# One more gate/up tile moved out of the attention filler, a thinner filler from unit 14 on, and three DMA issues moved, in a transformer block on one Trainium2 core

## The chip, the cores and the metric

The kernel runs on one core of a Trainium2 chip. The metric is the device time of one execution in microseconds. Before the change three runs gave 1046.39, 1044.46 and 1044.87 us, so the median is 1044.87 us. Engines are named as in the profile: PE (TensorE matmuls), PEld (its weight loads), DVE (VectorE), ACT (ScalarE), POOL (GpSimd) and SP (SyncE, here only the issuer of most DMAs).

## What is computed

x is 2048 tokens by 640 features in float32. After a layer norm, two branches run on the same normed x, and both are added to x:

```
xn  = layernorm(x)
A   = softmax(q k^T / sqrt(20), causal, window 256) v @ wo     # 32 heads of 20
B   = (gelu(xn @ w_gate) * (xn @ w_up)) @ w_down               # 640 -> 1728 -> 640
out = x + A + B
```

## The kernel before, in words

Nearly every dense product is done as three float32r products of split operands (high by high, low by high, high by low), so a product of 128 output rows by 512 tokens over 640 features is 15 matmuls. Tokens are cut into 4 chunks of 512. The gate and up weights are cut into 14 tiles of 128 columns; tile 13 holds the last 64 columns of both.

The program has three long stages, each with an order written out by hand.

**Attention (`attention`, L818).** Heads go in 8 groups of four, so there are 32 units (group, chunk). Each unit is 14 slots. In a slot a fixed pattern puts instructions out: `exp_piece` (L558) in every odd slot up to 11, two pieces at a time, computes scores on PE into the tile `ps_e` (pool `psx`, two buffers, shared with `ps_o`) and ACT takes the exponential out of it (L574); `max_pair` (L488) in slots 0, 0 again, 5 and 9 computes scores for a coming unit on PE into `ps_m` (pool `psm`, four buffers), and DVE scans them for row maxima (L517); `av_unit` (L593) in slot 0 multiplies the probabilities of the unit before by v into `ps_o`, and ACT copies it out (L621, L622); POOL clears the masked parts of the probabilities (L587, L590). `max_end` (L531) comes in slot 7: it turns the row maxima of the next unit by a matmul (`ps_n`, L534), ACT copies them to `mr` (L536), and a DMA on ACT's queue writes them as two more rows of the query tile `qs` (L537), which the next unit's `exp_piece` reads as part of its contraction from its slot 1 on.

The rest of PE's time in a slot is filled from a generator, `filler` (L705), which gives out matmuls of other work one by one: the remaining q and k projections (`proj_qk`, L240), the v projections (`proj_v`), and whole gate/up tiles (`gate_up_fill`, L661). A 512-column matmul counts 1, a 320-column one 0.65. `pull_fill(RATE / NS)` (L863) takes 30.9 of them per unit, 2.2 per slot. `sets` (L700) lists what the filler holds: q/k tiles 1 to 4, then gate/up tiles 0, 1 and 2 (`range(1, NFA)` with `NFA = 3`); tile 13 is loaded with it and multiplied just behind the attention. A filler gate/up tile is 2 x 15 x 4 = 120 matmuls. Its followers are ACT's L669, L670 and L679, and DVE's L675, L683 and L690, placed a few slots behind by `defer` and by the table `LAG`; a q/k tile has L277, L273, L255 and L259 as its followers.

**Gate/up (`gate_up_pair`, L954).** The tiles from `NFA` on are done here, each in two calls, one per pair of chunks. A call uses sums of token chunks and of weights, which leave 54 matmuls of 512 columns per call, 108 per tile. The attention's leftovers (normalising its output, sums of down-projection weights) are worked off in between by `work` (L1121).

**Down and output projection (from L1414).** 8 token blocks of 256, each with 9 weight quads and one remainder step. `fetch` (L1031) loads a weight quad into `stg`; after the first ones it is issued by ACT, from the table `plan` (L1425). `load_step` issues the loads of activations on SP, four steps ahead; `drain` (L1262) adds the products to x and stores a block through SP, which issues in order.

Of the kernel before, what the change touches and what calls it, by code (L numbers as in the profile page):

```python
# [28 lines left out]
SR = 3 * DH  # L29
QROWS = 64 + SR  # L30
NS = 14
RATE = 30.9
LAST = 8
V1_SLOT = 169
MXD = 7
KSLOT = 9
LAG = 3, 5, 4, 4, 4, 4, 3, 3, 4, 3, 2, 1, 1, 1
NFA = 3
HD = D // 2
HR = 5  # L40
NQD = 9
# [26 lines left out]
def block_kernel(ctx, tc, x, wqk, wv, wgu, wdo, wdl, out):  # L68
    nc = tc.nc
# [128 lines left out]
    now = [None]  # L198

    def at(slot, fn, *a):  # L200
        acts.setdefault(slot, []).append((fn, a))
# [3 lines left out]
    def late(fn, *a):  # L205
        if now[0] is None or now[0] < NS:
            fn(*a)
        else:
            lates.append((fn, a))
# [6 lines left out]
    def lag():  # L216
        return 1 if now[0] is None or now[0] < NS else LAG[now[0] % NS]

# [119 lines left out]
    NQ, NK = 3, 4  # L338
    qs = [st1.tile([128, 4, C], BF, name=f"qs{i}") for i in range(NQ)]
# [191 lines left out]
    def max_end(u):  # L531
        nm = maxes.pop(u)
        ps = psm.tile([128, 128], F32, name="ps_n", tag="mx")
        nc.tensor.matmul(ps, nm.rearrange("p z a j b -> p (z a j b)"), identb, start=True, stop=True)  # L534
        mr = ap.tile([32, 128], BF, name="mr", tag="mr")
        nc.scalar.activation(mr, ps[0:32], AF.Copy)  # L536
        late(lambda: nc.scalar.dma_start(qs[u % NQ][SR:SR + 2].rearrange("p j t -> p (j t)"), mr))  # L537

    def pieces(c):
        b = 4 * c  # L540
# [159 lines left out]
    sets = [("qk", 1), ("qk", 2), ("qk", 3), ("qk", 4), ("gu", 0)]  # L700
    sets += [("gu", f) for f in range(1, NFA)] + [("gu", NF - 1)]
    pools = (wp, None), (hp, 2)
# [110 lines left out]
    def pull_fill(n):  # L813
        debt[0] += n
        while debt[0] > 0:
            debt[0] -= next(fill, 1.0)

    def attention():  # L818
        now[0] = -1
        load_stack(0)  # L820
        load_stack(1)
        load_stack(2)
        for i, (p, k, half) in enumerate((p, k, half) for p in range(NC // 2) for k in range(2) for half in range(2)):
            for j, fn in enumerate(x_sums(p, k, half)):
                m = 10 * i + j
                at(NS * (XS0 + m // XSN) + m % XSN, fn)
        for i in range(12):
            now[0] = i - 13
            for fn, a in tick():
                fn(*a)  # L830
            if i == 0:
                pull_max(1, now[0])
                pull_fill(RAMP)
                pull_max(1, now[0])
                debt[0] -= RAMP
            elif i % 2 == 0:
                pull_max(2, now[0])
            flush()
            pull_fill(2 * RAMP)
        pull_fill(GAP)  # L840
        for u in range(NU + 1):
            for i in range(NS):
                T = now[0] = NS * u + i
                for fn, a in tick():
                    fn(*a)
                if i in (0, 5, 9) or T == 3:
                    pull_max(2, T)
                if i == 0 and u:
                    if u == NU:
                        pull_fill(LAST)  # L850
                    av_unit(u - 1)
                    flush()
                    pull_max(2, T)
                if i % 2 and i < 12 and u < NU:
                    exp_piece(u, i - 1)
                    if i == 1 and u:
                        pull_fill(1)
                        debt[0] -= 1
                    exp_piece(u, i)
                flush()  # L860
                if u + 3 < NU and i in (KSLOT, 12):
                    load_stack(u + 3, (int(i == KSLOT),))
                pull_fill(RATE / NS)  # L863
        while acts:
            now[0] += 1
            for fn, a in tick():
                fn(*a)
            flush()
        now[0] = None
        run(fill)  # L870
        assert not acts
# [156 lines left out]
    def four(t):  # L1028
        return t.rearrange("p k (h n) -> p (k h) n", h=2)

    def fetch(kind, q, where="stg", eng=nc.sync):  # L1031
        if where == "wr":
            ts = [wrp.tile([128, KT, 128], F32, name="wr", tag="wr").rearrange("p k m -> p (k m)") for _ in range(2)]
        elif where != "stg" and where != "at":
            ts = [tp.tile([128, D], F32, name=f"b{n}{q}", tag=f"x{n}{where}") for n in "hl"]
        if where != "stg" and where != "at":
            for i, t in enumerate(ts):
                nc.sync.dma_start(t, wdo[q][:, i])
            staged[kind, q] = [(t.rearrange("p (h n) -> p h n", h=2), slice(2 * i, 2 * i + 2)) for i, t in enumerate(ts)]
            return  # L1040
        pool, bufs = (rp3, 3) if where == "stg" else (cp, 3)
        t = pool.tile([128, 4, HD], F32, name="stg", tag=where, bufs=bufs)
        eng.dma_start(t, four(wdo[q]) if kind == "b" else wtd[q])
        if kind == "t" and q in borrow:
            staged[kind, q] = [(t[:, i:i + 1], slice(i, i + 1)) for i in range(4)]
        else:
            staged[kind, q] = [(t, slice(0, 4))]
# [95 lines left out]
    NP = S // 256  # L1143
# [118 lines left out]
    def drain(p, ps, xt):  # L1262
        xs = {(r, h): xt[:, 2 - r, h * HD - HD:h * HD] for r in (1, 2) for h in (1, 2)}
        rows = {1: slice(256 * p + 128, 256 * p + 256), 2: slice(256 * p, 256 * p + 128)}

        def add(r, h, i, eng=nc.vector):
            eng.tensor_tensor(out=xs[r, h], in0=i, in1=xs[r, h], op=OP.add)  # L1267

        def store(r, h=None):
            cs = slice(h * HD - HD, h * HD) if h else slice(0, D)  # L1270
            nc.sync.dma_start(out[rows[r], cs], xt[:, 2 - r, cs])

        b = {i: ps[i][:, 0:HD] for i in ps}
        if p == 0:
            for bank, r, h in ((2, 1, 1), (3, 1, 2), (4, 2, 1), (8, 2, 2)):
                add(r, h, b[bank])
                if h == 2:
                    store(r)
            return
        a = copies.pop(p)  # L1280
        both = cp.tile([128, 2, HD], F32, name="u2", tag="r13")
        q, c5 = both[:, 0], both[:, 1]
        if p < NP - 1:
            nc.scalar.activation(c5, b[5], AF.Copy)
        if p == NP - 1:
            add(1, 1, b[2])
            add(1, 1, a)
            store(1, 1)
            sub(q, b[6], a, OP.add)
            add(1, 2, q)  # L1290
            sub(q, b[7], q, OP.add)
            add(2, 1, q)
            add(2, 2, q)
            add(2, 1, b[4])
            store(2, 1)
            add(1, 2, b[5])
            add(2, 2, b[5])
            store(2, 2)
            add(1, 2, b[3])
            store(1, 2)  # L1300
            return
        add(2, 1, b[4])
        sub(q, b[6], a, OP.add)
        add(1, 2, q)
        sub(q, b[7], q, OP.add)
        add(1, 2, b[3])
        add(1, 2, c5)
        add(1, 1, a)
        store(1)
        add(2, 1, q)  # L1310
        add(2, 2, c5)
        add(2, 2, q)
        if p == 1:
            add(2, 2, b[8])
        store(2)
# [7 lines left out]
    order.__enter__()  # L1323
    raws_w = load_gu(NFA)
    banks = [psg.tile([128, C], F32, name="ps_g", tag=f"g{i}") for i in range(4)]
# [104 lines left out]
    def prepare(n):  # L1430
        for op in plan.get(n, "").split():
            kind, q = op[1], int(op[-1])
            if op[0] == "f":
                fetch(kind, q, eng=nc.scalar)
            elif op[0] == "s":
                sum_quad(q)
            elif op[0] == "p":
                kind, q, i = "t", int(op[1]), int(op[2])
                for raw, t, dst in parts(kind, q):
                    raw, dst = (raw, dst) if q in borrow else (raw[:, i:i + 1], slice(i, i + 1))  # L1440
                    if q not in borrow or t is quads["b", borrow[q] + i]:
                        nc.scalar.activation(t[:, 0, dst], raw, AF.Copy)
                        sub(t[:, 1, dst], raw, t[:, 0, dst].bitcast(F32))
            else:
                (high_quad if op[0] == "h" else low_quad)(kind, q)
        if n == 2:
            nc.scalar.activation(w13[:, 0], raw13, AF.Copy)
            sub(w13[:, 1], raw13, w13[:, 0].bitcast(F32))
        if n == 0:
            fetch("b", 5)  # L1450
            fetch("b", 6)
# [76 lines left out]
```

## Time and profile before

| what | us |
|---|---|
| median of three runs | 1044.87 |
| the profiled execution, device time | 1045.72 |
| its span in the trace | 1044.0 |
| PE busy | 1033.4 |
| DVE busy | 741.7 |
| ACT busy | 527.5 |
| POOL busy | 385.5 |

The profiled execution is 0.85 us over the median, and 1.7 us of its device time lie outside its span. A line of the timeline reads: start, duration, engine, source line, operation, output tile <- input tiles, shape, count, and in square brackets the idle time before it with what ended that. Matmul durations overlap: one row's duration is not the step from one matmul to the next, which is read from the starts. A line of the chain reads: start, duration, what, count.

### The profile page before, as it was taken

Reading aid. Unit: us, or ns where it says so; the run is one execution under the profiler, and the core shown is the slowest. Engines: PE = TensorE matmul, PEld = TensorE weight load, DVE = VectorE, ACT = ScalarE, POOL = GpSimd, SP = SyncE. Lnnn points to the kernel's source line nnn. Section 1 sums busy time; section 2 is a strip of 40 time slices with the busy share of each in tenths; the row PEclk is TensorE's granted clock in tenths of the full one; section 3 lists DMA queues with packets and bytes.
Section 4 is the critical chain, followed back from the end, with each engine's and each line's share of the span. In section 5 each row is a group of like instructions: output and inputs, shape, how many; then the busy total and the mean of one; then the engine's idle time right before and its main releaser. Section 6 shows DMA issues by size and latency. Waiting matters only on the chain.

```text
span 1044.0 us, 25563 instructions
## 1 busy us (share of the span) xinstructions
PE 1033.4 (99%) x9393; PEld 834.3 (80%) x9393; DVE 741.7 (71%) x2018; ACT 527.5 (51%) x1120; POOL 385.5 (37%) x623
## 2 busy tenths in 40 slices
PE   9999999999999999999999999999999999999998
PEld 8887666666777666666678888888888999999998
DVE  7755666677655676677736778776555889888887
ACT  4534766767666666666675322233224554433332
POOL 5122788888755787766461111101110000000000
PEclk9999999999999999999999999999999999999999
DMA  5552356554633354343325576662216874433333
GB/s 211 180 157 70 110 157 183 165 181 142 183 98 100 114 168 138 103 134 110 99 77 193 188 244 212 253 250 105 78 59 242 263 249 136 138 127 123 117 121 106
DMA packets 102150, 158.74 MB, mean 152 GB/s; under 512 B 14172, under 2 KB 55260, under 8 KB 102024
## 3 DMA queue, kind: packets, MB, share of 16 engines
q1 hardware_dynamic: 99640, 150.94, 44.5%
q10 hardware_dynamic: 2384, 6.16, 1.7%
q8 instruction: 74, 1.21, 0.5%
q14 instruction: 52, 0.43, 0.1%
HBM read 101.78 MB, written 54.92 MB: 150 GB/s over the span
## 4 chain that ended last, share of the span: by engine, by line
PE 90%; DVE 5%; ACT 2%; DMA 2%; issue 1%; POOL 0%; ACTq 0%; DVEq 0%; SPq 0%
PE ps_g L972 22%; PE ps_d L108 20%; PE ps L1244 20%; PE ps_e L572 8%; PE ps_v L108 7%; PE ps_o L615 5%; PE ps_m L507 5%; DVE junk L517 2%; PE ps_g L108 1%; DMA stg<-wdo 1%; ACT wb L1058 1%; PE ps_d L356 1%; PE ps_t L185 0%; DVE wb L1077 0%; DMA qs<-qd 0%
## 5 line engine op out<-in xcount | busy, mean ns | idle before, releaser
L517 DVE CUSTOM_DVE_ANT_0 junk<-ps_m,mask 128x320 bf16<-128x320 f32 (+2 forms) x512 | 243.0, 475 | 128.9 <-PE ps_m L507 71.0
L574 ACT ACTIVATE P<-ps_e 128x512 f32<-128x512 f32 (+2 forms) x384 | 198.7, 572 | 68.3 <-PE ps_e L572 67.8
L1244 PE MATMUL ps<-wb,at 128*128 128x320 f32 x999 | 156.4, 309 | 0.8 <-DVE xr L1267 0.8
L1244 PEld LDWEIGHTS ps<-wb,at 128*128 128x128 f32 x999 | 148.9, 188 | 1.5 <-issue 1.0
L587 POOL TENSOR_SCALAR_AFFINE_SELECT P<-P 128x256 f32<-128x256 f32 (+1 forms) x192 | 94.5, 494 | 73.2 <-ACT P L574 70.0
L572 PE MATMUL ps_e<-qs,ks 124*128 124x128 bf16 (+2 forms) x704 | 118.3, 278 | 0.1
L108 PE MATMUL ps_d<-xh,wqh 128*128 128x512 f32 x310 | 99.0, 422 | 0.2 <-ACT xh L193 0.2
L108 PE MATMUL ps_d<-xl,wqh 128*128 128x512 f32 x310 | 98.5, 422 | 0.0
L108 PE MATMUL ps_d<-xh,wql 128*128 128x512 f32 x310 | 97.6, 418 | 0.0
L101 POOL TENSOR_TENSOR wql<-wr,wqh 128x640 fp32r<-128x640 f32 x12 | 19.2, 1608 | 195.6 <-PE ps_g L972 171.1
L1244 PE MATMUL ps<-wt,at 128*128 128x320 f32 x552 | 88.9, 309 | 0.0
L572 PEld LDWEIGHTS <-ks 124*128 124x128 bf16 x704 | 49.5, 98 | 49.0 <-issue 33.4
L1244 PEld LDWEIGHTS ps<-wt,at 128*128 128x128 f32 x552 | 82.9, 188 | 0.1
L590 POOL TENSOR_SCALAR_AFFINE_SELECT P<-P 128x512 f32<-128x512 f32 (+1 forms) x144 | 76.7, 541 | 16.2 <-ACT P L574 16.2
L1198 ACT ACTIVATE at<-ss 128x512 fp32r<-128x512 f32 x59 | 37.3, 632 | 84.5 <-DVE ss L1077 84.5
L615 PE MATMUL ps_o<-P,v 64*32 64x320 f32 (+4 forms) x2816 | 74.2, 347 | 0.0
L259 POOL TENSOR_TENSOR pt<-r,pt 128x512 bf16<-128x512 f32 x40 | 46.8, 1169 | 64.6 <-ACT pt L255 57.0
L615 PEld LDWEIGHTS ps_o<-P,v 64*32 64x32 f32 x2816 | 50.8, 106 | 21.5 <-issue 0.9
L507 PE MATMUL ps_m<-ks,qs 60*64 60x320 bf16 (+3 forms) x1472 | 64.6, 260 | 3.4 <-DVE mx L517 1.5
L108 PEld LDWEIGHTS ps_d<-xh,wqh 128*128 128x128 f32 x310 | 56.0, 189 | 10.4 <-issue 1.6
L507 PEld LDWEIGHTS <-qs 60*64 60x64 bf16 x1472 | 29.1, 105 | 43.8 <-issue 35.6
L108 PEld LDWEIGHTS ps_d<-xh,wql 128*128 128x128 f32 x310 | 56.0, 189 | 10.1 <-issue 0.9
(195 smaller groups left out, 1967.4 us busy)
## 6 DMA issues: line engine op xcount, KB each, us to landing
hd<-he SPq DMA_DIRECT2D x50, 256.0 KB
hr<-hd SPq DMA_DIRECT2D x48, 256.0 KB
wr<-wgu SPq DMA_DIRECT2D x27, 320.0 KB
qs<-qd SPq DMA_DIRECT2D x64, 120.0 KB
ks<-kd SPq DMA_DIRECT2D x64, 120.0 KB
xi<-x SPq DMA_DIRECT2D x16, 320.0 KB
qs<-qd SPq DMA_DIRECT2D x64, 80.0 KB
ks<-kd SPq DMA_DIRECT2D x64, 80.0 KB
```

The source lines that it names most:

```text
L108: nc.tensor.matmul(ps, a(k), b(k), start=n == 0, stop=n == 3 * nk - 1)
L259: nc.gpsimd.tensor_tensor(out=pt[:, l, :], in0=r, in1=pt[:, 1, :], op=OP.subtract)
L507: nc.tensor.matmul(ps[64 * h:64 * h + 64, col:col + w], q[rows, j, q0:q0 + 64], ks_, start=True, stop=True, tile_position=(64 * r, 64 * h))
L517: nc.vector.tensor_tensor_reduce(out=junk[:, 0:n], in0=ps[:, 320 - n:320], in1=mask[:, 320 - n:320], scale=1.0, scalar=NEG, op0=OP.add, op ...
L572: nc.tensor.matmul(ps[:, col:col + n], k[0:QROWS, j, kc:kc + 128], q[0:QROWS, j, q0:q0 + n], start=True, stop=True)
L574: nc.scalar.activation(pt[:, j, lo:hi], ps[:, lo:hi], AF.Exp, scale=SCALE)
L587: nc.gpsimd.affine_select(out=a, in_=a, pattern=[[0, n], [1, 128]], compare_op=OP.is_ge, fill=0.0, base=0, channel_multiplier=-1)
L590: nc.gpsimd.affine_select(out=a, in_=a, pattern=[[0, n], [-1, 128]], compare_op=OP.is_ge, fill=0.0, base=-1, channel_multiplier=1)
L615: nc.tensor.matmul(os[r][32 * j:32 * j + 32, qa:qb], v[rows, w0_:w0_ + 32], pt[rows, j, col + qa - q0:col + qb - q0], start=r not in begun ...
L972: nc.tensor.matmul(ps, i, j, start=first and n == 0, stop=n == len(work) - 1, skip_group_check=True)
L1198: nc.scalar.activation(hi[:, 3:7], s, AF.Copy)
L1244: nc.tensor.matmul(ps[bank][:, 0:HD], *work[bank][j], start=bank not in begun, stop=final[p, bank] == n and j == len(work[bank]) - 1, skip ...
```

## The change

Three things change. First, `NFA` goes from 3 to 2: gate/up tile 2 leaves the filler and is done by `gate_up_pair`, as the first of 11 tiles there instead of 10; with 120 matmuls less to give out, the filler's rate goes from 30.9 to 24.2 per unit from unit 14 on. Second, the DMA of the maxima row is put in slot 13 of the unit, instead of slot 7. Third, in the last stage the quads listed in `plan` are fetched by GpSimd and not by ACT, and the stores of `drain` are issued by GpSimd and not by SP, but for the last block.

```diff
+TURN, RATE2 = 14, 24.2
...
+MRSLOT = 13
...
-NFA = 3
+NFA = 2
...
-        late(lambda: nc.scalar.dma_start(qs[u % NQ][SR:SR + 2].rearrange("p j t -> p (j t)"), mr))
+        issue = lambda: nc.scalar.dma_start(qs[u % NQ][SR:SR + 2].rearrange("p j t -> p (j t)"), mr)
+        if now[0] < 0:
+            issue()
+        else:
+            at(now[0] - now[0] % NS + MRSLOT, issue)
...
-                pull_fill(RATE / NS)
+                pull_fill((RATE if u < TURN else RATE2) / NS)
...
-            nc.sync.dma_start(out[rows[r], cs], xt[:, 2 - r, cs])
+            (nc.sync if p == NP - 1 else nc.gpsimd).dma_start(out[rows[r], cs], xt[:, 2 - r, cs])
...
-                fetch(kind, q, eng=nc.scalar)
+                fetch(kind, q, eng=nc.gpsimd)
```

Lines of the changed kernel stand 2 to 6 lines lower than those of before; L574 is L580 there, L108 is L110, L537 is L539.

On PE, in a unit of the second half, this is the piece from the last score product of slot 5 to the first of slot 7 before (`ps_e` are the score products, `ps_d` the filler, `ps_n` the turned maxima):

```order
L572 LDWEIGHTS ks_182
L572 MATMUL ps_e<-qs_178,ks_182 128x256
L108 MATMUL ps_d<-xh_79,wqh 128x512 x5
L534 LDWEIGHTS nm_183
L534 MATMUL ps_n<-identb,nm_183 128x128
L572 LDWEIGHTS ks_181
L572 MATMUL ps_e<-qs_178,ks_181 128x256
```

And the same piece in a unit of the changed kernel's second half:

```order
L578 LDWEIGHTS ks_182
L578 MATMUL ps_e<-qs_178,ks_182 128x256
L110 MATMUL ps_d<-xl_80,wqh 128x512 x2
L110 MATMUL ps_d<-xh_77,wqh 128x512
L536 LDWEIGHTS nm_183
L536 MATMUL ps_n<-identb,nm_183 128x128
L578 LDWEIGHTS ks_181
L578 MATMUL ps_e<-qs_178,ks_181 128x256
```

Three filler matmuls stand between the two pairs of score products in this place, where five stood; in other units there are four before, or four after.

On ACT, a whole unit of the second half before reads as follows, from the copies of `ps_o` in slot 0 to the unit's end (`P` are the exponentials, `gs` and `he` the followers of a filler gate/up tile):

```order
L621 ACTIVATE ob<-ps_o 128x512
L622 ACTIVATE P<-ps_o 128x512
L574 ACTIVATE P<-ps_e 128x384 x4
L574 ACTIVATE P<-ps_e 128x256 x2
L536 ACTIVATE mr<-ps_n 32x128
L574 ACTIVATE P<-ps_e 128x256 x2
L537 DMA qs_178<-mr 2x16x128
L574 ACTIVATE P<-ps_e 128x512 x2
L669 ACTIVATE gs<-ps_d 128x512
L670 ACTIVATE he<-ps_d 128x512
L574 ACTIVATE P<-ps_e 128x512 x2
L679 ACTIVATE he<-he 128x512
```

And a unit of the changed kernel's second half:

```order
L627 ACTIVATE ob<-ps_o 128x512
L628 ACTIVATE P<-ps_o 128x512
L580 ACTIVATE P<-ps_e 128x512 x6
L538 ACTIVATE mr<-ps_n 32x128
L580 ACTIVATE P<-ps_e 128x512 x2
L675 ACTIVATE gs<-ps_d 128x512
L676 ACTIVATE he<-ps_d 128x512
L580 ACTIVATE P<-ps_e 128x512 x4
L685 ACTIVATE he<-he 128x512
L539 DMA qs_176<-mr 2x16x128
```

The DMA of the maxima row stands behind all the exponentials of the unit, and `gs` and `he` stand before four exponentials where two were left. A gate/up chunk is 30 filler matmuls: at 30.9 per unit its followers come at nearly the same slot in every unit, at 24.2 the slot changes from unit to unit.

On ACT, the first fetches of the last stage stand before among the splits of weights (`wb`, `wt`) and of activations (`at`):

```order
L1043 DMA stg<-wdo 128x1280
L1058 ACTIVATE wb_12653<-stg 128x1280
L1058 ACTIVATE wt_12655<-stg 128x1280
L1186 ACTIVATE at<-hr 128x512
L1043 DMA stg<-wtd_112 128x1280
L1043 DMA stg<-wtd_114 128x1280
L1058 ACTIVATE wb_12692<-stg 128x1280
```

On POOL, the changed kernel's program ends with these, where before it had nothing behind the splits of the gate/up stage:

```order
L1049 DMA stg<-wdo 128x1280 x2
L1049 DMA stg<-wtd_112 128x1280
L1049 DMA stg<-wtd_114 128x1280
L1049 DMA stg<-wtd_113 128x1280
L1049 DMA stg<-wtd_108 128x1280
L1277 DMA out<-xr 128x640 x2
L1049 DMA stg<-wtd_109 128x1280
L1049 DMA stg<-wtd_110 128x1280
L1049 DMA stg<-wtd_111 128x1280
L1277 DMA out<-xr 128x640 x12
```

Nine fetches and fourteen stores thus wait in one queue in which nothing else stands.

## The prediction

> **What bounds the kernel now.** I read the page's busy times first, then the stages as windows, then the chain that ended last, and the waits in the stage that the change thins out.
>
> ```profile
> span 1044.0 us, 25563 instructions
> PE 1033.4 (99%) x9393; PEld 834.3 (80%) x9393; DVE 741.7 (71%) x2018; ACT 527.5 (51%) x1120; POOL 385.5 (37%) x623
> PEclk9999999999999999999999999999999999999999
> ```
>
> PE is busy for 99% of the span, at a clock granted in full all the way. Rows of matmuls overlap, so 99% could hide small gaps; the stages and the steps between matmuls say more. The windows are the attention's units 1 to 13, its units 14 to 31, the gate/up stage and the last stage (columns: window, its length, PE, PEld, DVE, ACT, POOL busy, clock, DMA share, GB/s).
>
> ```profile
> 102.10:287.10 185.00, 183.82 (x2452) 123.72 (x2448) 125.22 (x466) 126.99 (x270) 150.32 (x254) 1.00 0.54 159
> 287.10:541.00 253.90, 252.19 (x3395) 173.81 (x3394) 163.37 (x602) 168.18 (x373) 171.40 (x293) 1.00 0.37 113
> 543.40:802.10 258.70, 258.70 (x1146) 213.97 (x1141) 177.24 (x294) 85.27 (x157) 28.93 (x20) 1.00 0.51 178
> 802.10:1044.00 241.90, 237.77 (x1616) 236.75 (x1614) 206.70 (x443) 100.25 (x179) 0.00 (x0) 1.00 0.47 159
> ```
>
> The second window holds the 18 units that get less filler: 253.9 / 18 = 14.1 us each. In it DVE, ACT and POOL are busy for 64%, 66% and 68%, so none of them is the bound on average. The steps of the matmuls come from the chain:
>
> ```profile
> 50.30 6.85 PE ps_d L108 x30
> ...
> 557.27 234.08 PE ps_g L972 x1032
> ...
> 835.99 204.71 PE ps L1244 x1391
> ```
>
> A filler matmul takes 6.85 / 30 = 0.228 us, a gate/up one 234.08 / 1032 = 0.2268 us, one of the last stage 0.1472 us. The last two rows are runs of hundreds of microseconds in which PE waits for nothing, so time leaves those stages only with matmuls. Next, the waits in the 18 units (who waits, for whom, total us, times, longest):
>
> ```profile
> PE ps_m L507 <- DVE mx L517: 1.1, 4, 0.4
> ACT P L574 <- PE ps_e L572: 40.8, 68, 1.5
> ACT ob L621 <- PE ps_o L615: 33.6, 16, 3.5
> ```
>
> PE is recorded as waiting 1.1 us there, always for DVE's scan of a maxima tile. ACT waits for PE, 40.8 us for scores alone. So this stage is bound by PE's own work, with cover for the other engines: 2.3 us per unit before ACT's exponentials.
>
> **Part 1: the tile.** Out of the filler go 2 x 15 x 4 = 120 matmuls at 0.228 us: -27.4 us, if PE stays the bound. Into the gate/up stage come 108 at 0.2268 us: +24.5 us. That stage runs as one chain of PE, and DVE has 81 us of idle time in it (258.70 - 177.24), so followers, sums and DMAs of the extra tile lie beside PE. Net -2.9 us. The tile's fetches by SP, its splits on ACT and POOL and its four stores go with it, into a stage where POOL is 11% and ACT 33% busy.
>
> **Part 2: what the thinner filler uncovers.** A unit should shrink from 14.1 us by 6.7 x 0.228 = 1.5 us to 12.6 us. DVE, 163.37 / 18 = 9.1 us per unit, POOL 9.5 and ACT 9.3 still fit, even before the tile's followers go out. So no engine takes over on average; the question is the short distances. The score pieces have two buffers, and these rows of PE, and of ACT below it, show how near they are:
>
> ```profile
> 482.81 0.61 PE L572 MATMUL ps_e<-qs,ks 124*128 124x128 bf16 x4
> 483.13 0.77 PE L108 MATMUL ps_d<-xl,wqh 128*128 128x512 f32 x2
> 483.74 0.62 PE L108 MATMUL ps_d<-xh,wqh 128*128 128x512 f32 x2
> 484.20 0.63 PE L572 MATMUL ps_e<-qs,ks 124*128 124x128 bf16 x4
> ```
> ```profile
> 483.31 1.09 ACT L574 ACTIVATE P<-ps_e 128x512 f32<-128x512 f32 x2 [1.08 <-PE ps_e L572]
> 484.28 0.60 ACT L669 ACTIVATE gs<-ps_d 128x512 f32<-128x512 f32 x1
> 484.76 0.62 ACT L670 ACTIVATE he<-ps_d 128x512 f32<-128x512 f32 x1
> 485.23 1.12 ACT L574 ACTIVATE P<-ps_e 128x512 f32<-128x512 f32 x2
> ```
>
> Two pieces start on PE at 482.81, ACT reads them from 483.31 to 484.40, and PE starts the next two at 484.20, 1.39 us after the first. The second of these needs the buffer that ACT lets go at 484.40, and begins half-way through a pair's 0.33 us, at about 484.36. So four filler matmuls between two pairs just cover ACT. With three, PE comes 0.23 us sooner and waits some 0.2 us. In the changed order such gaps (slots 5 to 7 and 9 to 11) have three or four, 24.2 / 7 = 3.46 on average, so about half are short: 2 x 0.5 x 0.2 = 0.2 us per unit. The gaps with `ps_m` in them (3 to 5, 7 to 9) are some 0.4 us longer and stay covered; slots 1 to 3 add at most 0.1 us. Upper end 0.3 x 18 = 5.4 us. Lower end 0: a wait moves the second piece back, which gives ACT the same time before the next pair, and the 40.8 us of waiting ACT say that it catches up. I take 0.15 us per unit, half of the upper end, because the only row of such a gap lies right on the edge: +2.7 us.
>
> Second, `gs` and `he` hold ACT for 0.95 us (484.28 to 485.23). Before, they come as here, ahead of a unit's last two exponentials or behind them, where no later score piece waits. In the changed order they drift: in a few units of the tail they stand ahead of four or six exponentials. A wrong place costs between 0 (a gap with `ps_m` behind it) and 0.75 us (0.95 less the 0.2 by which a short gap, 1.39 - 0.23, exceeds two exponentials, 0.97), over 8 chunks 0 to 6 us; ACT's idle share makes me put most of it inside the 2.7 us, and the rest into a rival.
>
> DVE's four recorded waits, 1.1 us, depend on the same drift; I keep them (bounds -1.1 to +2).
>
> **Part 3: the maxima row.** The DMA leaves ACT's row between two exponentials and stands where ACT waits for `ps_o` anyway. The gain is nothing that PE sees. The risk is its distance to its reader, shown by PE's rows from slot 0 to slot 1:
>
> ```profile
> 472.12 0.37 PE L507 MATMUL ps_m<-ks,qs 60*64 60x64 bf16 x12
> ...
> 475.76 0.39 PE L572 MATMUL ps_e<-qs,ks 124*128 124x128 bf16 x2
> ```
> ```profile
> SPq L482 <- DMA qs<-mr: 9.2, 6, 2.5
> ```
>
> From the scan products of slot 0 to the first score piece are 3.64 us, and slot 13's filler adds 0.3 to 0.5 us. SP was held by this DMA for at most 2.5 us at a time. So it arrives with over a microsecond in hand; I take 0, with bounds of 0 and, were half of the 32 units late by 0.5 us, +8 us. Nothing is queued behind it but the copies of `ps_o`, and it waits for an `mr` that was written six slots before.
>
> **Part 4: the last stage's issues.**
>
> ```profile
> 817.65 0.40 ACTq L1043 DMA_DIRECT2D stg<-wdo  x1
> ...
> 823.45 1.26 ACT L1058 ACTIVATE wb<-stg 128x1280 fp32r<-128x1280 f32 x1
> ...
> 827.05 1.74 ACTq L1043 DMA_DIRECT2D stg<-wtd  x2
> 828.84 1.27 ACT L1058 ACTIVATE wb<-stg 128x1280 fp32r<-128x1280 f32 x1 [1.99 <-DVE wt L1077]
> ```
> ```profile
> 835.99 14.31 PE L1244 MATMUL ps<-wb,at 128*128 128x320 f32 x96 [0.81 <-DVE xr L1267]
> ```
> ```profile
> SPq L1271 <- DVE xr L1267: 100.0, 12, 12.5
> ```
>
> ACT stands for 1.99 us behind two fetches that wait for a staging buffer; the split of a quad, DVE's low part and then DVE's additions `xr` come that much later, and PE waits 0.81 us for the first of them. On GpSimd, idle in this stage, the fetches hold up nobody. That can return the 0.81 us, and SP's loads no longer stand behind stores (100 us of waiting), which PE doesn't feel, since it has no other wait here. I take -0.8 us; ends -1.0 and, if a load by GpSimd comes late, +3. A fetch issued at 817.65 is read without a wait 5.8 us later, so there is room for a slower issue.
>
> The Trainium skill speaks against this part: its page DMA: Bandwidth & Descriptors, section Issuing engine by pattern, gives simple loads and stores to SP, and the section Latency and other measured facts puts the first byte of a GpSimd DMA at about 1 us against 0.6 us for one of SP or ACT. By that page the 0.8 us would be an estimated 0.4 us. No trace here shows a DMA of GpSimd.
>
> **The sum.** 1045.72 - 27.4 + 24.5 + 2.7 + 0 - 0.8 = 1044.7 us against the profiled execution, -1.0 us. That execution is 0.85 us over the median, so the forecast for the median is 1043.9 us.
>
> **The rivals.**
> - *All of it is covered*: ACT's 40.8 us and the alternation keep PE from waiting. Then -2.9 - 0.8 = -3.7, with DVE's waits gone too -4.8: about 1040.7 us. For it: PE hardly waits in the units now. Against it: the gap at 484.20 has no slack.
> - *The score buffers become the bound* (slower): short gaps and drifting `gs`/`he` add up in the 18 units. Price 5.4 us plus half of the 6 us, with -3.7: +4.7, 1049.6 us. It decides from 0.32 us of new waiting per unit on (5.8 us in all, 3.7 to undo the gain and 2.1 to pass 0.2%). For it: ACT's row in the changed order; against it: 34% idle time of ACT.
> - *A late DMA* (slower): the maxima row after its 4 us, or a fetch by GpSimd after its 5.8 us: +3 to +8 us, some 1049 us.
> - *The tile isn't cheaper where it goes* would need a wait in the gate/up stage, which has none: left out.
>
> **How the numbers follow.** The forecast, 1042.5 to 1046 us, has 0.44; everything covered 0.29; score buffers 0.19; late DMA 0.08. The range of 1040.0 to 1049.2 us takes in the forecast, the covered case and the nearer half of the slower ones. A measurement of this kernel can tell about 0.2% (2.1 us) from no change: faster means under 1042.8, slower over 1047.0. The covered case is faster, with a little of the forecast: 0.36. The two slower cases and a little of the forecast: 0.26. The rest, 0.38, is the same.
>
> **What would show it.** Right: the run of L978 in the chain has 108 more matmuls at 0.227 us; the units from 14 on take 12.6 to 12.9 us; waits of `ps_e` for ACT of 0.1 to 0.3 us each, two or so per unit; PE's wait at the start of the second token block of the last stage is gone. Wrong: units of 13 us or more, a PE wait for `qs<-mr` at slot 1, ACT waiting for `stg` behind a GpSimd issue, or units at 12.6 us without any waits (then the covered case holds).

## The result and the profile after

The changed kernel is slower. Its median is 1058.58 us of five runs (1054.95 to 1060.53), beside 1044.95 us for the kernel before in the same series; the ratio is 1.0119, with a 95% interval of 1.0101 to 1.0136. The forecast was 1043.9 us, with a range that ended at 1049.2 us. The profiled execution took 1060.53 us. Of the five runs the one with a mean granted clock of 1.0 took 1054.95 us and the four at 0.996 to 0.998 took 1057.18 to 1060.53 us; a run of e7 at 0.753, 1250.09 us long, is in no ratio below.

The first lines of its page:

```profile
span 1058.7 us, 25550 instructions
...
PE 1040.7 (98%) x9381; PEld 836.7 (79%) x9381; DVE 747.2 (71%) x2029; ACT 527.2 (50%) x1120; POOL 393.4 (37%) x638
...
PEclk9999999999999999999999999999999999999999
```

PE has 12 matmuls less in this execution and is busy 7.3 us longer. The digit row of the clock looks as before, but a slice is 26 us long and hides what is shown below. The same four stages as windows (units 1 to 13, units 14 to 31, gate/up, last stage; columns: window, length, PE, PEld, DVE, ACT, POOL busy, clock, DMA share, GB/s):

```profile
102.10:297.20 195.10, 188.16 (x2452) 126.24 (x2448) 125.87 (x467) 127.56 (x270) 149.79 (x254) 0.98 0.52 151
297.20:532.70 235.50, 231.59 (x3263) 153.44 (x3259) 154.11 (x590) 160.45 (x359) 165.80 (x286) 1.00 0.39 115
535.10:818.20 283.10, 283.10 (x1259) 234.48 (x1250) 193.00 (x319) 92.58 (x172) 31.15 (x21) 1.00 0.50 170
818.20:1058.70 240.50, 237.19 (x1616) 236.69 (x1614) 205.20 (x441) 99.87 (x179) 12.57 (x23) 1.00 0.49 158
```

Against the windows of before that is +10.1, -18.4, +24.4 and -1.4 us, +14.7 in all, the difference of the spans. The tile costs in gate/up what it was to cost, the thinner units give back less than they were to (18.4 of 27.4 us), and 10 us are lost in units 1 to 13, where only the maxima row was moved. Two of these units make 8.1 of the 10.1 us: unit 5 takes 19.32 us instead of 15.15, unit 9 takes 18.15 instead of 14.17. The chain that ended last names that loss, here first that of before and then that of after (`qs<-qd` is the load of the queries of a unit, with the keys `ks<-kd` its stack loads; the scan products that read them first go into `ps_m`):

```profile
162.23 4.11 DMA qs<-qd
```
```profile
149.61 2.17 DMA qs<-qd
...
165.72 3.30 DMA qs<-qd
...
226.69 3.19 DMA qs<-qd
...
258.71 2.22 DMA qs<-qd
...
286.48 2.95 DMA qs<-qd
...
549.03 269.28 PE ps_g L978 x1188
818.30 237.09 PE ps L1250 x1615
```

Before, one stack load stands in the chain of these units; after, PE's end hangs on five. The gate/up row has 1188 matmuls instead of 1032 at 269.28 / 1188 = 0.2267 us (the run of the chain begins at another place than before, so that its count grows by more than the 108 of the tile), so the price of a gate/up matmul has not changed.

**Where the 10 us are made.** The timeline around 160 us: the DMA issues of SP, in the second fence that of ACT, in the third PE.

```profile
156.45 2.33 SPq L484 DMA_DIRECT2D ks<-kd  x6
161.17 0.83 SPq L236 DMA_DIRECT2D wr<-wqk  x2
162.11 1.33 SPq L270 DMA_DIRECT2D qd<-pt  x2
163.54 2.89 SPq L484 DMA_DIRECT2D qs<-qd  x6
```
```profile
158.47 0.62 ACTq L539 DMA_DIRECT2D qs<-mr  x1
```
```profile
167.68 0.27 PE L509 MATMUL ps_m<-ks,qs 60*64 60x256 bf16 x1 [1.83 <-DMA qs<-qd]
169.16 0.47 PE L509 MATMUL ps_m<-ks,qs 60*64 60x256 bf16 x15 [1.22 <-DMA qs<-qd]
```

SP has put out six loads by 158.78 and then stands until 161.17, though the next two loads (`wr`) have nothing to do with the maxima row. The rows of SP's program say why:

```
184 L636 DMA sd_99<-ob 4x512 [waits DMAHW7_49]
185 L484 DMA ks_182<-kd_91 40x1024 [waits DMAHW0_49]
...
190 L484 DMA ks_182<-kd_91 60x1024 [waits DMAHW5_49]
191 L236 DMA wr<-wqk 128x640 [waits DMAHW6_49]
```

In this program, as it is built, the DMAs of SP and ACT share eight completion semaphores and take them in turn, one round of eight after the other. The one that SP skips ahead of row 184 was given to ACT's maxima row, and row 191, eight places on from ACT's row in that round, may not be issued until that DMA has landed. ACT issues the row at 158.47; SP comes to row 191 at 158.78, long before the row has landed, and stands until 161.17. Behind it stand the `qd` stores and the `qs` loads, which come some 2 us later than before (the last is issued by 166.4 instead of 164.4), and PE waits 1.83 and 1.22 us for them. Then something happens that the row of digits doesn't show: windows just before and just behind these waits, and at the second such place.

```profile
165.70:169.60 3.90, 0.85 (x18) 0.45 (x18) 0.77 (x2) 1.57 (x3) 2.23 (x4) 1.00 0.77 227
169.60:173.00 3.40, 3.40 (x16) 2.32 (x14) 1.92 (x8) 1.99 (x5) 1.59 (x2) 0.50 0.43 129
231.10:234.50 3.40, 3.40 (x12) 2.37 (x11) 1.43 (x6) 2.71 (x6) 1.29 (x2) 0.50 0.19 62
```

For 3.4 us PE gets half its clock, which costs another 1.7 us at each of the two places. The waits of units 1 to 13, of SP's queue and of PE:

```profile
SPq L484 <- DMA qs<-mr: 15.8, 8, 3.3
...
SPq L270 <- DMA qs<-mr: 2.4, 1, 2.4
...
SPq L236 <- DMA qs<-mr: 2.4, 1, 2.4
```
```profile
PE ps_m L509 <- DMA qs<-qd: 5.9, 7, 1.8
...
PEld L578 <- DMA qs<-mr: 0.3, 1, 0.3
```

The same waits of these units before the change:

```profile
SPq L482 <- DMA qs<-mr: 7.6, 4, 2.5
```
```profile
PE ps_m L507 <- DMA qs<-qd: 0.6, 1, 0.6
```

SP waits 20.6 us for the row instead of 7.6; for the row itself PE's weight load waits 0.3 us, and the product not at all. So the row is not late for its reader. What it holds up is SP.

**Where the thinner units lose.** A short gap of unit 24, between two pairs of score pieces, now with three filler matmuls:

```profile
436.37 0.61 PE L578 MATMUL ps_e<-qs,ks 124*128 124x128 bf16 x4
...
436.68 0.53 PE L110 MATMUL ps_d<-xl,wqh 128*128 128x512 f32 x1
...
436.86 1.09 ACT L580 ACTIVATE P<-ps_e 128x512 f32<-128x512 f32 x2 [1.04 <-PE ps_e L578]
...
437.05 0.63 PE L110 MATMUL ps_d<-xh,wqh 128*128 128x512 f32 x2
...
437.52 0.85 PE L578 MATMUL ps_e<-qs,ks 124*128 124x128 bf16 x4
```

The pairs start 1.15 us apart instead of 1.39. ACT lets the second buffer go at 436.86 + 1.09 = 437.95, and the second pair lasts 0.85 us instead of 0.61: a wait of 0.24 us, too short for the view of waits, which has only a fraction of this loss.

### The profile page after: what moved, and what is told of

Same layout as the page of the kernel before. It is cut to its first block, busy times and chain, and to the rows that moved or that the text cites. A ratio compares the mean times of both kernels' runs of the same rounds, so it can differ in the third digit from the quotient of the medians.

```text
span 1058.7 us, 25550 instructions
## 1 busy us (share of the span) xinstructions
PE 1040.7 (98%) x9381; PEld 836.7 (79%) x9381; DVE 747.2 (71%) x2029; ACT 527.2 (50%) x1120; POOL 393.4 (37%) x638
## 4 chain that ended last, share of the span: by engine, by line
PE 90%; DVE 4%; ACT 3%; DMA 2%; issue 1%; SPq 0%; POOL 0%; DVEq 0%; ACTq 0%
PE ps_g L978 25%; PE ps L1250 22%; PE ps_d L110 16%; PE ps_e L578 8%; PE ps_v L110 6%; PE ps_o L621 6%; PE ps_m L509 5%; DVE junk L519 2%; ACT P L580 2%; DMA qs<-qd 2%; PE ps_g L110 1%; PE ps_d L358 1%; PE ps_t L187 0%; DMA xi<-x 0%; SPq L484 0%
## 5 line engine op out<-in xcount | busy, mean ns | idle before, releaser
L580 ACT ACTIVATE P<-ps_e 128x512 f32<-128x512 f32 (+2 forms) x384 | 198.7, 572 | 60.3 <-PE ps_e L578 59.0
L578 PE MATMUL ps_e<-qs,ks 124*128 124x128 bf16 (+2 forms) x704 | 123.7, 280 | 2.3 <-ACT P L580 0.7
L110 PE MATMUL ps_d<-xh,wqh 128*128 128x512 f32 x270 | 90.0, 430 | 0.2 <-ACT xh L195 0.2
L110 PE MATMUL ps_d<-xl,wqh 128*128 128x512 f32 x270 | 87.4, 427 | 0.0
L110 PE MATMUL ps_d<-xh,wql 128*128 128x512 f32 x270 | 86.9, 424 | 0.0
L509 PE MATMUL ps_m<-ks,qs 60*64 60x320 bf16 (+3 forms) x1472 | 67.0, 260 | 9.2 <-DMA qs<-qd 6.1
L509 PEld LDWEIGHTS <-qs 60*64 60x64 bf16 x1472 | 30.6, 105 | 50.4 <-issue 36.6
L1277 POOL DMA_DIRECT2D out<-xr x14 | 7.6, 544 | 167.9 <-DVE xr L1273 162.7
L1007 ACT ACTIVATE hr<-hr 128x512 f32<-128x512 f32 x22 | 13.9, 632 | 111.2 <-DVE hr L981 111.2
```

The lines of the kernel that those rows point to most:

```text
L110: nc.tensor.matmul(ps, a(k), b(k), start=n == 0, stop=n == 3 * nk - 1)
L509: nc.tensor.matmul(ps[64 * h:64 * h + 64, col:col + w], q[rows, j, q0:q0 + 64], ks_, start=True, stop=True, tile_position=(64 * r, 64 * h))
L578: nc.tensor.matmul(ps[:, col:col + n], k[0:QROWS, j, kc:kc + 128], q[0:QROWS, j, q0:q0 + n], start=True, stop=True)
L580: nc.scalar.activation(pt[:, j, lo:hi], ps[:, lo:hi], AF.Exp, scale=SCALE)
```

## The experiments

Theory A: the moved row is the loss, through the semaphore that SP shares with ACT. Its rival B: the thinner filler is the loss. Ratios are to the kernel before on the same chip, with 95% intervals.

### One part at a time: e1, e2, e3, e4

e1 is the kernel before with the row in slot 13; e2 is the changed kernel with the row put back; e3 is the kernel before with the tile and the thinner rate alone; e4 has the last stage's issues alone.

```diff
 e1, to before:  +MRSLOT = 13, and the row's issue by at(...) as in the change
 e2, to after:   -MRSLOT = 13, and the row's issue by late(...) as before, in slot 7
 e3, to before:  +TURN, RATE2 = 14, 24.2     -NFA = 3   +NFA = 2
 e4, to before:  the changed lines of store() and of plan's fetch
```

> The kernel before with one edit: the DMA of the maxima row in slot 13. Theory A (the moved DMA is the loss: SP, which shares completion semaphores with it, is held until it has landed, loads of queries come late, PE waits in units 1 to 13 and its clock is halved behind the longest waits): 8 to 13 us slower than before, some 1053 to 1058 us, with units 1 to 13 taking about 195 us instead of 185. Theory B (the loss is in the thinner filler of units 14 to 31, and the long units early on are chance): within 1 us of before, 185 us in units 1 to 13.

> The changed kernel with one part undone: the DMA of the maxima row back in slot 7. Theory A: it loses the 10 us of units 1 to 13 and some waits behind them, and comes to 1044 to 1049 us, so that what is left against before is the score buffers' waits against 2.9 us of matmuls saved and 1.5 us of the last stage. Theory B: it stays within 2 us of the changed kernel, 1057 to 1060 us.

> The kernel before with only the tile moved and the thinner filler from unit 14 on (row in slot 7, last stage as before). Theory A: 1.5 us over the changed kernel with the row in slot 7, so some 1045 to 1050 us; the 18 thinned units at 13.0 us each. Theory B: 1055 us or more.

> The kernel before with only the last stage's loads and stores by GpSimd. Both theories: 0.8 to 1.6 us faster than before, 1043.3 to 1044.2 us, the wait of 0.81 us at the second token block gone. If GpSimd's DMAs were part of the loss, it is slower than before by over 1 us.

Measured: e1 1051.93 us, 1.0063 (1.0043 to 1.0083); e2 1049.79 us, 1.0034 (1.0022 to 1.0046); e3 1049.97 us, 1.0041 (1.0029 to 1.0053); e4 1045.61 us, 0.9989 (0.9977 to 1.0001); before 1045.95 us. Here the kernel before lies at 1047 to 1049 us, with a mean clock of 0.998, in 10 of its 26 runs, so all four ratios are some 0.1% low (e14 and e11 repeat e1 and e3 beside a kernel before without this).

Both theories hold in part: with that 0.1% the row and the thinner filler each cost 5 to 8 us, and the last stage's issues neither cost nor save anything that shows. e1 stays under the 8 to 13 us that theory A gave it, e2 is 0.8 us over its range, and e4's saving of 0.8 to 1.6 us did not come. e1's units 1 to 13 take 190.4 us; with the row in slot 7 (e2, e3) they take 185.0 and 184.9. In e4's last stage, the window and PE's waits:

```profile
801.20:1044.90 243.70, 238.51 (x1617) 236.80 (x1615) 206.21 (x443) 99.18 (x179) 12.57 (x23) 1.00 0.48 158
```
```profile
PE ps L1244 <- DVE xr L1267: 1.5, 2, 0.8
```

The wait for `xr` is still there, and the stage is longer than before (241.90). In e1, e11 and e12, where ACT issues the fetches and SP the stores as before, PE has no such wait and the stage takes 240.6 us; the changed kernel, with GpSimd's issues, has none either, in 240.5 us. So it comes and goes from one execution to the next, and GpSimd's issues don't decide it.

### Is it the row, or what stands behind it: e5, e6, e9

```diff
 e5, to e1:   -nc.scalar.dma_start(qs...)   +nc.gpsimd.dma_start(qs...)
 e6, to e1:   -MRSLOT = 13                  +MRSLOT = 10
 e9, to e1:   -nc.scalar.dma_start(qs...)   +nc.sync.dma_start(qs...)
```

> The kernel before, with the maxima row in slot 13 as in e1, but issued by GpSimd, which does not use the completion semaphores that SP and ACT share. Theory A (the row in slot 13 hurts because SP's next loads, on the same semaphore, stand behind it): SP's wait for the row (e1: 13 waits, 23.0 us) vanishes, units 1 to 13 take 184 to 186 us again, the time is within 1.5 us of the kernel before. Rival (the row itself comes late, or what stands in slot 13 is in ACT's way): like e1, 190 us for units 1 to 13 and 4 to 8 us above the kernel before.

> The kernel before, with the maxima row issued in slot 10 by ACT. Theory A: the loss depends on what SP has in its queue at that moment (the loads of slot 9 stand there, those of slot 12 not yet), so it lies between before and e1: 1 to 4 us above before, SP's wait for the row 12 to 22 us. Rival (the row's distance to its reader decides): three slots of room, 3.3 us more than in e1, so no loss, within 1 us of before.

> As e1 (the kernel before with the maxima row in slot 13), but the row is issued by SP itself, so that no DMA of SP has to wait on a semaphore for one that ACT has yet to issue. Theory A (SP runs ahead of ACT, and the DMA that is next on the row's semaphore stands until ACT has come to slot 13 and the row has landed): no hold of 2 to 3 us on SP any more, except where the row itself waits for its data; units 1 to 13 take 184.5 to 187 us, the time is within 2 us of before. Rival (in slot 13 the row reaches its reader late, as it did by GpSimd in e5): PE waits for the row at the first score products, 188 us or more for units 1 to 13, 3 to 10 us above before.

Measured: e5 1068.77 us, 1.0244 (1.0228 to 1.0260); e6 1046.11 us, 1.0025 (1.0013 to 1.0037); e9 1065.65 us, 1.0204 (1.0187 to 1.0221). e6 is where theory A put it: SP waits 15.9 us for the row in the whole program, and 2.2 us are lost. e5 and e9 are far worse than e1, which theory A did not expect. In both SP no longer waits for the row to land, and PE's wait at the scan products for `qs<-qd` is gone, as the theory had it; but now PE waits for the row itself, in e5 6.8 us (and 9.6 us for `ps_n`, of which more below), in e9, over the whole program:

```profile
PEld L577 <- DMA qs<-mr: 22.9, 17, 3.4
...
PE ps_e L577 <- DMA qs<-mr: 17.5, 16, 3.0
```

On SP the row stands in order behind stores and stack loads that wait, and slot 13 leaves no room for that. So e5 and e9 swap one loss for another and don't decide between A and a row that is late; e14 and e15 do.

### A DMA that nobody reads: e12, e13, and e14 (e1 again)

```diff
 e12, to before:
+        if now[0] >= 0:
+            at(now[0] - now[0] % NS + MRSLOT, lambda: nc.scalar.dma_start(dz[u], mr))
 e13: the same line with nc.gpsimd
```

`MRSLOT` is 13; `dz` is a scratch buffer in DRAM; the maxima row stays in slot 7.

> The kernel before, row in slot 7 as it was, and in slot 13 ACT issues one more DMA of 8 KB, a copy of the row into a scratch buffer in DRAM that nobody reads. Theory A (SP's next DMA on the same completion semaphore stands until this one has landed): SP waits 20 to 35 us in all for the added DMA, PE waits for the stack loads, units 1 to 13 take 187 to 196 us, 3 to 9 us over before, as in e1. Rival (e1's loss comes from the row's short way to its reader): nobody reads the added DMA, so units 1 to 13 take 184.5 to 186 us and the time is within 1.5 us of before.

> As e12, but GpSimd issues the added DMA. Theory A: GpSimd's DMAs do not use the semaphores of SP and ACT, nobody waits for this one, POOL has the room: within 1.5 us of before, no wait of SP for it. If an added DMA in slot 13 as such is the cost (its transfer, its issue): 3 us or more over before.

> e1 once more (row in slot 13 by ACT): 1.004 to 1.009 of before, units 1 to 13 189 to 196 us, SP waiting 20 to 34 us for the row, PE 3 to 7 us for stack loads and under 1.5 us for the row.

Measured: e12 1045.13 us, 1.0009 (1.0001 to 1.0018); e13 1059.87 us, 1.0149 (1.0136 to 1.0162); e14 1051.00 us, 1.0068 (1.0055 to 1.0081). Both expectations of theory A for e12 and e13 fell; e12's time is the one that the rival gave. But the rival's reason, a row that is late for its reader, is not what costs e1 its time: in e14, which is e1 again and loses 6.9 us, the view of waits has neither a product nor a weight load of PE that waits for the row, while the scan products wait 3.9 us for `qs<-qd`. Why e12 loses nothing is shown by its own trace, SP's issues and ACT's:

```profile
158.04 0.87 SPq L236 DMA_DIRECT2D wr<-wqk  x2
159.01 1.34 SPq L270 DMA_DIRECT2D qd<-pt  x2
161.03 2.91 SPq L484 DMA_DIRECT2D qs<-qd  x6
```
```profile
158.13 0.32 ACTq L541 DMA_DIRECT2D dz<-mr  x1
```

The added DMA has another place in the round of eight. SP's next user of its semaphore is not `wr` but the first `qs` load, four places later, and SP comes to it when the added DMA is about to land: 0.7 us of standing instead of 2.4, and over the program 7.1 us for `dz` instead of the 20 to 35 expected. So e12 shows that a DMA in slot 13 is no loss in itself; it did not make the hold that it was to make.

e13's loss has another cause. The operation that ends DVE's maxima in one unit, and all of its kind in the program (count, then min/median/max in ns):

```profile
137.05 4.82 DVE L528 TENSOR_SCALAR nm<-mx 128x16 bf16<-128x16 f32 x1
```
```profile
L528 DVE TENSOR_SCALAR nm<-mx x32: 174/175/5316, 75.5 to 536.1; 128x16 bf16<-128x16 f32 x32
```

In the kernel before its longest is 990 ns. Meanwhile POOL runs eight instructions without a break, from 136.58 to 141.83; the last two are

```profile
140.62 1.21 POOL L594 TENSOR_SCALAR_AFFINE_SELECT P<-P 128x512 f32<-128x512 f32 x2
```

and DVE goes on when they end. Three more operations of this kind take 3.8 to 5.3 us in e13, and each ends within 0.1 us of POOL's last. PE then waits for `ps_n` and its clock is halved (0.97 over units 1 to 13, which take 200.6 us). e5 shows the same operation four times with 3.9 to 5.5 us. The Trainium skill, SBUF — State Buffer, section SBUF: two separate sides, says that VectorE, in some of its modes, and GpSimd share one port pair under an exclusive lock and that the loser blocks fully; the trace agrees in kind, with 4.82 us for 0.17 us of work, though the page has the lock held for one instruction and this wait went on over eight. Whether this operation ran in such a mode, no run shows. That GpSimd's extra issue (0.51 us each) brought POOL into that unbroken stretch is argued, not shown.

### Only there, and everywhere but there: e15, e16

```diff
 e15, to e1:  -if now[0] < 0:    +if now[0] < 0 or now[0] // NS in (4, 8):     late(...), the old place
 e16, to e1:  -if now[0] < 0:    +if now[0] // NS not in (4, 8):               late(...), the old place
```

> e1 (row in slot 13 by ACT), but in units 4 and 8 the row stays in slot 7. Theory A (the loss is made in the two places where SP, held at the row's semaphore, comes late with the stack loads of the next unit): units 5 and 9 take 14.1 to 14.8 us instead of 18, units 1 to 13 under 187 us, the time within 2 us of before although the row is moved in all other units. Rival (the row in slot 13 costs a little in every unit): 4 to 7 us over before, as e1.

> The kernel before, with the row in slot 13 in units 4 and 8 alone. Theory A: these two rows carry the loss, 3 to 4 us each: units 5 and 9 take 17 to 19 us, 4 to 8 us over before, as e1. Rival (a little in every unit): 2 of 32 units, under 1 us over before.

Measured: e15 1045.42 us, 1.0014 (1.0002 to 1.0027); e16 1046.37 us, 1.0019 (1.0009 to 1.0030). Units 1 to 13 of e14 and of e15, and SP's wait in e15:

```profile
102.13:294.42 192.29, 187.71 (x2452) 126.02 (x2448) 125.68 (x467) 127.21 (x270) 149.73 (x254) 0.98 0.52 154
```
```profile
102.14:287.92 185.78, 184.27 (x2452) 124.02 (x2448) 125.31 (x467) 126.80 (x270) 149.97 (x254) 1.00 0.54 159
```
```profile
SPq L483 <- DMA qs<-mr: 21.2, 14, 2.4
```

With the row back in its old place in two units, and in slot 13 in all others, some 5 of e14's 7 us are gone; units 5 and 9 take 14.96 and 14.13 us instead of 18.05 and 17.91. SP still waits 21.2 us for the row at the stack loads, 28.1 us in all where e14 has 30.5, but at places where nobody needs its next loads soon. That refutes a small price in every unit. But e16, these two rows alone, costs 2 us and not the 4 to 8 of theory A:

```profile
155.33 5.21 SPq L235 DMA_DIRECT2D wr<-wqk  x2
160.64 1.38 SPq L269 DMA_DIRECT2D qd<-pt  x2
162.12 2.77 SPq L483 DMA_DIRECT2D qs<-qd  x6
```

Here too SP is held at `wr` until 160.2. It had reached it earlier, though, only the second `wr` load was held, and the `qs` loads go out 0.6 us earlier than in e14 (162.73), 1.4 us earlier than after the change (163.54). PE's products wait 1.0 us for them in all units together, and its clock stays whole. Alone the two rows lose 2.0 us (e16), the others 1.1 us (e15), together 6.9 us (e14), so the loss needs both. What the others add in this unit is another place in the round of eight, in which the row holds the first `wr` load and not the second, so that one load more comes behind the hold; whether that is all of it is not shown.

### The thinner filler: e7, e8, e10, e11 (e3 again)

```diff
 e7, to e3:   pull_fill(TAB[i]) from unit 14 on, TAB = 1.3, 2.1, 2.1, 1.2, 1.2, 2.1, 2.1, 1.2, 1.2, 2.1, 2.1, 1.9, 1.9, 1.7
 e8, to e3:   TAB = 2.0, 1.3, 1.3, 2.2, 2.2, 1.3, 1.3, 2.2, 2.2, 1.3, 1.3, 1.9, 1.9, 1.8
 e10, to e3:  TURN = 6, TAB = 1.3, 2.14, 2.14, 1.55, 1.55, 2.14, 2.14, 1.55, 1.55, 2.14, 2.14, 2.06, 2.06, 1.79
```

> e3 (the tile alone, row in slot 7) with the same 24.2 of filler per unit from unit 14 on, but spread unevenly over the slots: 4.2 in the gaps between score pairs that hold nothing else (1 to 3, 5 to 7, 9 to 11), 2.4 in those with scan products. Theory (the score buffers are the bound in the short gaps only): the 5 us of extra time at the score products falls to 1 to 2 us, time 3 to 4 us under e3, 1045.5 to 1047 where before is at 1045.9. Rival (ACT's order, with the splits gs and he in front of exponentials, sets the waits wherever the filler stands): no gain, within 1 us of e3's 1050.

> The opposite of e7: the same 24.2 of filler per unit, 2.6 in the short gaps, 4.4 in those with scan products. Theory (short gaps): three gaps in each of 18 units short by another 0.1 to 0.25 us, so 5 to 13 us of further waits at the score products, 1055 to 1062. Rival (ACT's order decides, not the place of the filler): within 1.5 us of e3's 1050.

> The tile alone, row in slot 7, but the 120 matmuls leave 26 units (from unit 6 on, 26.25 of filler each) and not 18, and the filler stands 4.3 in the short gaps and 3.1 in those with scan products. Theory (only short gaps under four matmuls cost): extra time at the score products 0 to 2 us, 0.5 to 1 us at the scan products, so the net saving of about 2 us less that: 1.5 us under to 1 us over before. Rival (each filler matmul taken out uncovers about a quarter of its time wherever it stands): like e3, 3 to 5 us over before.

> e3 once more (the tile alone, thinned as in the change, row in slot 7), beside e10 on the same chip, since a few units of the kernel before had a halved clock where e3 was timed: 1.0035 to 1.0055 of before, 235 us for units 14 to 31.

Measured: e7 1047.97 us, 1.0035 (1.0022 to 1.0049); e8 1054.41 us, 1.0097 (1.0084 to 1.0111); e10 1048.93 us, 1.0047 (1.0033 to 1.0060); e11 1049.94 us, 1.0057 (1.0044 to 1.0069). The distances from the start of one matmul to the start of the next, summed from the trace by what stands before and behind (units 14 to 31, us; in brackets the number of steps; scan products are those into `ps_m`):

| kernel | filler to filler | score to score | filler to score | scan to scan | filler to `ps_n` |
|---|---|---|---|---|---|
| before | 113.1 (474) | 27.9 | 19.1 | 15.9 | 3.6 |
| e11 | 85.7 (354) | 33.4 | 20.6 | 16.9 | 3.7 |
| e7 | 85.4 (354) | 30.6 | 21.3 | 17.5 | 3.7 |
| e8 | 85.5 (354) | 38.6 | 22.7 | 14.8 | 3.6 |
| e10 | 93.5 (395) | 29.0 | 21.5 | 15.0 | 5.4 |

In e11 the 120 steps save their 27.4 us in full, and 8.1 us come back: 5.5 between score products, 1.5 ahead of them, 1.0 at the scan products. All of the growth between score products lies where nothing but filler stands between two pairs of score pieces: the 50 runs of four score products behind such short gaps take 20.9 us in e11 and 15.7 before, the 28 behind gaps with scan products 8.6 and 8.7. In e11 24 of the 50 gaps hold two or three filler matmuls, before 8. The windows of e11's units 14 to 31 and last stage show what is left:

```profile
287.27:522.13 234.86, 231.23 (x3264) 153.25 (x3260) 153.99 (x590) 160.20 (x359) 165.83 (x286) 1.00 0.38 115
807.53:1048.10 240.57, 237.25 (x1616) 236.76 (x1614) 205.02 (x441) 100.85 (x179) 0.00 (x0) 1.00 0.48 158
```

The place of the filler matters as the short gaps would have it: taken out of them (e8) the score steps grow by another 5.2 us, put into them (e7) they shrink by 2.8. But e7 gains 2 us on e11 and not 3 to 4, and e10, with 26 units thinned by less, is far from the 0 to 2 us of waiting that theory expected: its waits ahead of score products and of `ps_n` take the place. There the rival's "about a quarter, wherever it stands" is the better figure. In the five longest steps ahead of a score product of each of e7 and e10, ACT stands behind `gs` and `he`, a weight split, the copy of `mr` or the copies of `ps_o`. Which of these orders could be mended at once was not tried. No version here is shown to beat the kernel before: e4's interval reaches 1.0001.

## Why the prediction was wrong

**Part 1, the tile: right.** -27.4 us of filler steps and +24.5 for gate/up were forecast; -27.4 (e11) and +24.4 were measured.

**Part 2, what the thinner filler uncovers: the mechanism right, the term mis-sized.** It was put at 2.7 us and measured 8.1 in e11. Its sign of being wrong, "units of 13 us or more", came true: 235.5 / 18 = 13.1 us. The price of a short gap, 0.2 us, was near (0.24 in unit 24, 0.15 on average over e11's 24 gaps of two or three matmuls), and so was "about half are short" (24 of 50). The step that failed is "I take 0.15 us per unit, half of the upper end": the score steps alone grew by 5.5 us, the upper end itself (5.4), and the waits ahead of the first score piece and at the scan products, 2.5 us, were not in the term. Against what the lower end of 0 rested on, ACT did not catch up, though its waits for scores fell from 40.8 to 24.4 us. So the rival "the score buffers become the bound" was this part's true course: it priced these waits at 8.4 us, and they are 8.1 in e11. How much of them is owed to the drift of `gs` and `he`, no run tells apart. DVE's waits were to stay at 1.1 us and are at 1.0.

**Part 3, the maxima row: wrong, and the larger part of the error.** That it "arrives with over a microsecond in hand" was near enough: after the change only weight loads ever wait for it, twice, 0.7 us in all. "Nothing is queued behind it but the copies of `ps_o`" was the failed step. Only ACT's queue was looked at; behind the row's semaphore stood SP's queue, behind that the `qs` loads, and behind those PE and its clock. The quoted row `SPq L482 <- DMA qs<-mr: 9.2, 6, 2.5` showed SP waiting for this DMA and was read only as a measure of how long the DMA takes. SP never reads that row's data, and that should have raised the question why it waits. The row costs 6 to 7 us alone (e1, e14) and 8 to 9 us on top of the other two parts (1.0119 against e2's 1.0034, which is some 0.1% low); that the upper bound was 8 us is chance, since it stood for another mechanism.

**Part 4, the last stage: a term without a cause.** The 0.8 us was a wait of one execution. It is absent in e1, e11 and e12 with the old issues and present in e4 with the new ones; what brings it is open. The feared late fetch by GpSimd cost PE nothing either: ACT waits 2.4 us for quads in that stage after the change, 1.4 before.

**The sum.** With the measured parts, 6.2 us for the tile (e11), 6.0 to 6.9 for the row (e1, e14) and none for the last stage, 1044.95 becomes 1057 to 1058 us; 1058.58 was measured. That the profile of the tile alone says +4.1 us in span (1048.1 less 1044.0) and the times +6.2 is for 1.3 of the 2.1 us due to the profiled execution of before, whose last stage was that much longer than in e11.

## What to carry to other kernels

Before a DMA is moved to a later place on one engine's queue, look in the view of waits for other queues that already wait for it though they don't read its data: these stand behind its completion semaphore, and a later issue can hold them up. What that costs is decided by how soon the loads behind are needed: 28.1 us of such waiting cost 1.1 us in e15, 30.5 us cost 6.9 in e14. An engine with a third of its time idle can still be the bound at a buffer with two places; count such gaps in the new order and multiply, and where most of them sit on the edge, take the upper end. A gain that rests on one wait in one profiled execution is worth nothing until a second execution shows it.

## What the hardware showed that was not expected

- In these programs DMAs issued by SP and by ACT take turns on eight completion semaphores, and the issue of one waits for the landing of the eighth before it, whichever engine issued that: SP stood for up to 3.3 us behind ACT's 8 KB row. These waits stand in the rows of the program; that the chip itself would ask for them, no run shows. By its place in that round a DMA of ACT in slot 13 made SP stand in the same unit for 2.4 us (after the change) or for 0.7 us (e12).
- PE's clock was halved for 3.4 us after two waits of 1.83 and 1.22 us that one matmul parted. The Trainium skill, TensorE: Matmul & The Clock Gate, Part 1: The HAM clock gate, names an idle window of about 3.4 us as the condition; here PE was busy for 0.85 of the 3.90 us before the drop, so an unbroken idle stretch of that length was not needed.
- A DVE operation of 0.17 us took 3.8 to 5.5 us, four times in e5 and four times in e13, while POOL ran instructions without a break, and ended when POOL's last did; PE waited about 10 us for `ps_n` in each (9.6 and 10.4).
